# A hand-written instruction planner counts longer instruction fetches and a shorter run of warm-up products, and lays the order of an attention and MoE kernel anew

## The chip, the cores and the metric

The kernel runs on one core of a Trainium2 chip. The metric is the device time of one execution in microseconds (us). Three runs of the kernel before gave 327.25, 327.46 and 327.77 us; the median is 327.46 us. One further execution was profiled; durations in this document come from such profiled executions.

## What is computed

Two layers follow each other. The first is attention with 8 batches, 8 heads and head size 64. Each batch has 32 global tokens and 512 local ones. A global token attends to all 544 tokens; a local token attends to the 32 global tokens and to the local ones at a distance of at most 32.

```python
s_g = scale * np.matmul(q_g, k_all.transpose(0, 1, 3, 2))
out_g = np.matmul(sm(s_g), v_all)
mask = np.abs(pos[:, None] - pos[None, :]) <= window          # window = 32
s_ll = np.where(mask, scale * np.matmul(q_l, k_l.transpose(0, 1, 3, 2)), -1000000000.0)
s_lg = scale * np.matmul(q_l, k_g.transpose(0, 1, 3, 2))
a_l = sm(np.concatenate([s_lg, s_ll], axis=-1))
out_l = np.matmul(a_l, np.concatenate([v_g, v_l], axis=2))
```

The second is a two-layer network over the 4352 token rows of width 512 that come out of the first:

```python
h = x @ w_in                                   # 512 -> 2048
g = h * np.clip(h + 3.0, 0.0, 6.0) / 6.0
return (g @ w_out).astype(np.float32)          # 2048 -> 512
```

## The kernel before, in words

**Work of a batch.** Attention of a batch comes as four pairs of 32-query strips and two global units. A pair takes scores on TensorE (L712 for batches 0 and 1, in 32x32 tiles; L699 later, in tiles of another shape), eight masked maxima on VectorE (L743), eight exponentials on ScalarE (L749), eight 128x128 transposes on TensorE (L758), one copy out of PSUM (L318), the product with the values (L776, 32-column weights) and on VectorE the normalization (L785, L786) and the transpose to the layout of the network (L799, into the tile xt). A global unit takes scores (L824, later L816), a maximum (L831, L832), two exponentials (L836, L837), five transposes (L847) and a copy; both units together take one product with the values (L857). Scores, of pairs and of global units alike, go through one PSUM tile s: the next scores wait until all readers of the last ones are done.

**Network of a batch.** Sixteen column tiles of the first matrix (L907, four matmuls of 128x512 each; in batch 0 in three parts of fewer tokens) go into one of three PSUM buffers m0 to m2; ScalarE takes relu (L918), VectorE the product with it (L914, into gts), which frees the buffer. For each of the four groups of 128 tokens the second matrix takes 16 matmuls of 128x512 in four groups of four (L934), into the same three buffers, copied out by ScalarE or VectorE (L942, L944) and stored by SP. The first L907 of batches 1 to 7 needs all of the batch's xt, so it waits for the batch's last L776 and the L785, L786 and L799 after it. L934 of the batch before can be laid between.

**Loads.** For batches from 2 on, q and k are loaded by DMAs that POOL issues into 32 partitions of rawq and rawk, and SP then issues DMAs inside the memory that copy them to 32 further partitions (a pair for rawq, a pair for rawk; three of the same kind for the global rows, gn). VectorE transposes them from there (L646 for q, L650 for k, four instructions each). POOL also loads v and copies it into vs (L542; ScalarE has some of these copies of batch 0 at L540). SP issues its DMAs in order: a store that waits for its copy holds back what is queued behind it.

**The order.** No order is written out. The kernel adds every step to one of some 50 streams of a planner (class Plan, L34 to L196) with a cost on each engine that may take it, and `lay` (L124) puts steps one after the other on a model of the engines' clocks: at each turn the engine that can start first takes, among the steps that are ready there, the one of lowest rank (the number beside the stream's name, L296 to L299). A step that ScalarE or VectorE may take goes to the one with the smaller end, where VectorE's end counts SPARE later. The order that results is emitted once and is fixed from then on; at run time an engine goes through its own list and waits where a semaphore makes it.

The planner also has an instruction fetch in its model. It counts TensorE's instructions, weight loads and matmuls alike, in blocks of 256 (BLOCK). When the count passes into a new block at a time `when`, the block after it is taken to be there some microseconds later (`self.fetched`, L179); a step that would pass the next border before that time has its rank raised by 20, so that others go first. The 100 products of zeros at the start (stream "pad", L996) have a cost of their own, which the model multiplies by SLOW before COLD (30 us).

Where this document speaks of a place in TensorE's list, it numbers weight loads and matmuls in order; the kernel has 8968 of them, in both versions.

Of the kernel before, what the change touches and what calls it, by code (L numbers as in the profile page):

```python
# [37 lines left out]
class Plan:  # L38
# [4 lines left out]
    BLOCK = 256  # L43
    COLD, SLOW = 30.0, 1.9
    SWITCH, ALONE = 0.097, 0.5
    SPARE, PHASES = 0.5, 9

    def __init__(self, pools, claims):
        self.count, self.fetched, self.mode = 60, 0.0, "full"
# [72 lines left out]
    def lay(self):  # L122
        at = self.at = {n: 0 for n in self.streams}
        clock = {}  # L124
        order = []
        total = sum(len(s) for s in self.streams.values())
        while len(order) < total:
            found, lone = [], []
            for n, ops in self.streams.items():
                if at[n] == len(ops):  # L130
                    continue
                op = ops[at[n]]
                t = self.ready(op, n)
                if t is None:
                    continue
                for e in op.on:
                    if e in op.holds and op.holds[e].end is None:
                        continue
                    start = max(t, clock.get(e, 0.0))
                    cost = self.cost(op, e, start)  # L140
                    rank = self.rank[n](at[n]) if callable(self.rank[n]) else self.rank[n]
                    rank += self.tune.get((n, at[n] * self.PHASES // len(ops)), 0.0)
                    if e == "PE":
                        cost += self.switch(op)
                        if self.stalls(op, start, cost - self.switch(op))[0] > 0.2:
                            rank += 20
                        if op.mode[0] != "full" and self.mode != "full":
                            rank -= 15
                        elif op.mode[0] != "full" and start - t < self.ALONE:
                            lone.append(len(found))  # L150
                    found.append((start, rank, start + cost, n, e))
            if not found:
                raise RuntimeError("no operation can be laid: " + ", ".join(f"{n} {at[n]}" for n in at if at[n] < len(self.streams[n])))
            if len(lone) == 1:
                start, rank, end, n, e = found[lone[0]]
                found[lone[0]] = (start, rank + 12, end, n, e)
            first = min(found)
            e = first[4]
            here = [f for f in found if f[4] == e and f[0] <= first[0] + 0.03]
            start, _, end, n, e = min(here, key=lambda f: (f[1], f[0]))  # L160
            op = self.streams[n][at[n]]
            if len(op.on) > 1:
                own = min(f[1] for f in found if f[3] == n)
                wanted = lambda f: f[4] != e and any(g[4] == f[4] and g[3] != n and g[1] < own and g[0] <= f[0] + 0.05 for g in found)
                start, end, e = min(((f[0], f[2], f[4]) for f in found if f[3] == n and not wanted(f)),
                                    key=lambda f: f[1] + (self.SPARE + self.tune.get(("spare " + n, at[n] * self.PHASES // len(self.streams[n])), 0.0)
                                                          if f[2] == "DVE" else 0.0))
            for b, p, i in self.choose(op, n)[1]:
                b.at, b.slot = p, i
                self.free[p][i] = None  # L170
            at[n] += 1
            if op.landing is not None:
                self.issued.setdefault(e, []).append(op.landing)
            if e == "PE":
                wait, when = self.stalls(op, start, self.cost(op, e, start))
                end += wait
                self.mode = op.mode[1]
                if self.count % self.BLOCK + op.n >= self.BLOCK:
                    self.fetched = when + wait + (7.0 if when < 40.0 else 5.2)  # L179
                self.count += op.n  # L180
            clock[e] = end
            op.end, op.engine = end + op.lat, e
            for b in op.reads:
                b.left -= 1
                b.free_at = max(b.free_at, op.end)
                if b.left == 0:
                    self.free[b.at][b.slot] = b.free_at
            order.append((start, n, op))
        return order
# [3 lines left out]
def kernel(  # L193
# [12 lines left out]
    nc = tc.nc  # L206
# [6 lines left out]
    NDFF = dff // P  # L213
    W = 32
# [12 lines left out]
    PARTS, CG = ((1,), (0,), (2, 3)), 4  # L227
# [38 lines left out]
    vs = tiles("vs", 2, [P, NU, NJ, H, D1], FP16)  # L266
# [16 lines left out]
    zero = tiles("zero", 1, [W, W], FP16)[0]  # L283
# [9 lines left out]
    aps = tiles("a", 1, [P, 2, 512], FP32, pp)  # L293

    plan = Plan(sizes, {})
    for name, rank in (("l0", 0), ("ld", 5), ("lq", -2), ("sh", 0), ("sq", 0), ("st", 3.5), ("g0", 0), ("ga", -9), ("first", -9), ("pad", -30), ("gc", -6), ("gd", 3), ("gp", 3.9), ("cast", -5), ("msk", lambda n: 1 if n < 9 else 1.25), ("tq", lambda n: 0 if n < 8 else 3), ("kg", 0.5), ("vs", 1.5), ("clr", 1),  # L296
                       ("s", 0.5), ("mx", lambda n: 1.2 if n < 33 else 2.7), ("ex", 1.9), ("t", -0.5), ("etc", 0), ("av", -0.7), ("nm", 0.7),
                       ("xp", -0.5), ("gx", 1),
                       ("mf", lambda n: 9 + n * 1e-3), ("ms", lambda n: 9 + (n + len(PARTS) * NDFF + 2) * 1e-3), ("t1", 0), ("gate", -0.7), ("ot", 3)):  # L299
        plan.stream(name, rank)  # L300
    for name in ("l0", "ld", "lq", "sh", "st", "g0", "ga", "sq"):
        plan.stream("dq" + name, 0 if name in ("l0", "ld", "lq") else -1)
# [690 lines left out]

    with tc.manual_schedule():
        clean = plan.add("first", Op(("DVE", 0.1), lambda: nc.vector.memset(zero, 0.0)))
        plan.add("pad", Op(("PE", 4.0), lambda: [nc.tensor.matmul(out=aps[0][0:W, 0, 0:2], lhsT=zero, rhs=zero[:, 0:2], start=True, stop=True) for _ in range(100)], [clean],  # L996
                           n=200, mode=("small", "small")))
        plan.add("first", Op(("DVE", 3.4), setup))
        plan.add("first", Op(("ACT", 2.2), lambda: nc.scalar.activation(out=mxs[1], in_=mxs[0], func=EXP)))
        loads(0, "l0")  # L1000
        v_loads(0, "l0")
        w_in_l = load_w_in()
        made["clear"] = plan.add("clr", Op(("POOL", 2.4), lambda: clear(nc.gpsimd, 1), [made["ident"]]))
        turn_qk(0)
        loads(1, "l0")
        if WORDS > 1:
            g_first(1)
        v_loads(1, "l0")
        w_out_l = load_w_out()
        for u in range(NU):  # L1010
            state[1]["vs"][u, 0][0].deps[0].deps.append(w_out_l[NDFF // 2])
        for b in range(2, B):
            loads(b, "l0" if b == WORDS else "lq")
            if b >= WORDS and (b - WORDS) % NG == 0:
                g_rest(b, "l0" if b == WORDS else "ld")
            v_loads(b, "ld")
            if b < WORDS:
                g_first(b)
        for b in range(B):
            if b:  # L1020
                turn_qk(b)
            pairs_of = [local(b, n, b == 0 and at % 2 == 1, b == 0 and at < HALVES)
                        for at, n in enumerate(range(NI // 2) if b else (1, 0, 2, 3))]
            for one in pairs_of[:HALVES]:
                next(one, None)
            for one in pairs_of:
                next(one, None)
            for s in range(2):
                globe(b, s)
            globe_values(b)  # L1030
        for b in range(B):
            moe_first(b)
            for j in ([i for part in PARTS for i in part] if b == 0 else range(NJ - (b == B - 1))):
                moe_second(b, j)
        moe_global()
        moe_second(B - 1, NJ - 1, 2)
        state[1]["g4"].deps[0].holds = {"POOL": made["strips"][-1][1]}
        for need, op in made["strips"]:
            if need:
                op.holds = {e: state[0]["turned"][need - 1][1] for e in ("ACT", "DVE")}  # L1040
        firsts = [op for b, i, op in units if b == 0 and i < NI]
        firsts[2].holds = {"PE": state[0]["turned"][0][0]}
        firsts[3].holds = {"PE": state[0]["summed"][0]}
        for b, i, op in units:
            at = b - 1 + (i - LEAD) / (NI + 2)
            if at > 0:
                op.deps.append(hold(at))
        for _, _, op in plan.lay():
            op.emit()
# [30 lines left out]
```

## Time and profile before

| what | value |
|---|---|
| median of 3 runs | 327.46 us (327.25 to 327.77) |
| the profiled execution, its own time | 328.56 us |
| its span | 326.8 us, so 1.76 us lie around it |
| granted TensorE clock | 1.00 in every 10 to 20 us up to 300 us, 0.98 after |
| busy in the span | TensorE 305.8 us, VectorE 258.4, ScalarE 238.3, POOL 157.7 |
| TensorE busy in 0 to 10, 10 to 20, 20 to 30, 30 to 40 us | 3.43, 6.05, 8.56, 7.67 us |
| TensorE busy in 40 to 50, 50 to 60 us | 10.00, 7.23 us |
| TensorE busy in each stretch from 60 to 300 us | all of it |

A line of a timeline gives the start in us, the time from the start of the first to the end of the last of the merged instructions, the engine, the line of the kernel, the operation, the tiles (written <- read), the shape and how many; in brackets the idle time before it and what ended it. "issue" there means that the engine waited for nothing that the profile shows. Matmuls are pipelined, so the time from one start to the next start is what a group costs; the ends overlap.

### The profile page before, as it was taken

The page shows a single profiled execution, that of the slowest core. Times are in us where ns is not written, and L with a number is a line of the kernel's source. Part 1 is how long each engine was busy: PE and PEld are TensorE (multiplying, and loading weights), DVE is VectorE, ACT ScalarE, POOL GpSimd, SP SyncE. Part 2 cuts the span into 40 slices and gives each one's busy share as a digit, 9 for nine tenths or more (in the row PEclk, how much of TensorE's full clock was granted, in tenths as well). Part 3 has the DMA queues.
Part 4 walks back from the last instruction along what each step waited for, and adds up shares of the span by engine and source line. Part 5 has one row for each costly group of instructions (what it writes and reads, how often), then busy time and mean ns, then how long its engine had stood idle before and what let it go on. Part 6 is the DMA issues. An engine that isn't in the chain of part 4 may idle for free.

```text
span 326.8 us, 11215 instructions
## 1 busy us (share of the span) xinstructions
PE 305.8 (94%) x4484; PEld 172.8 (53%) x4484; DVE 258.4 (79%) x913; ACT 238.3 (73%) x550; POOL 157.7 (48%) x205
## 2 busy tenths in 40 slices
PE   4477898799999999999999999999999999999995
PEld 4356784454555545555555555555455545556654
DVE  7788996789989897989998999889989985742210
ACT  7999678557895788868876997699759965643221
POOL 9999999029955935665009944963900000000000
PEclk9999999999999999999999999999999999999999
DMA  8999999959952995199949993999111012011223
GB/s 201 180 215 190 188 212 170 230 152 178 200 85 66 140 184 138 46 111 160 217 118 99 226 138 48 148 157 174 33 35 34 2 34 67 0 34 32 65 53 79
DMA packets 104821, 39.54 MB, mean 121 GB/s; under 512 B 91648, under 2 KB 97536, under 8 KB 104768
## 3 DMA queue, kind: packets, MB, share of 16 engines
q0 software_dynamic: 91392, 16.91, 63.9%
q1 hardware_dynamic: 12832, 21.78, 26.8%
q8 instruction: 35, 0.57, 0.7%
q10 hardware_dynamic: 544, 0.13, 0.2%
q14 instruction: 18, 0.15, 0.2%
HBM read 35.13 MB, written 8.91 MB: 135 GB/s over the span
## 4 chain that ended last, share of the span: by engine, by line
PE 86%; POOL 5%; DMA 3%; DVE 2%; issue 2%; ACT 0%; POOLq 0%
PE m L934 37%; PE m L907 35%; PE t L758 4%; DMA xt<-in_q_l_dram 3%; PE a L776 3%; PE s L699 3%; PE t L847 1%; POOL vs L542 1%; PE s L816 1%; POOL v L308 1%; PE a L857 1%; PE s L712 1%; POOL win L308 1%; DVE qt L590 1%; DVE kt L595 1%
## 5 line engine op out<-in xcount | busy, mean ns | idle before, releaser
L934 PE MATMUL m<-wout,gts 128*128 128x512 f16 (+1 forms) x560 | 130.8, 373 | 1.8 <-issue 1.8
L907 PE MATMUL m<-xt,win 128*128 128x512 f16 (+2 forms) x640 | 121.0, 338 | 2.2 <-DVE gts L914 1.2
L914 DVE SCALAR_TENSOR_TENSOR gts<-t,m 128x512 f16<-128x512 f32 x136 | 92.1, 682 | 34.4 <-ACT t L918 33.1
L918 ACT ACTIVATE t<-m 128x512 f32<-128x512 f32 x136 | 81.2, 597 | 34.5 <-PE m L907 31.4
L907 PEld LDWEIGHTS <-win 128*128 128x128 f16 x704 | 70.4, 114 | 48.0 <-issue 3.8
L542 POOL COPY vs<-v 32x1056 f32<-32x1056 f32 (+4 forms) x91 | 81.7, 898 | 29.1 <-DMA v<-in_v_l_dram 24.8
L749 ACT ACTIVATE ex<-sm,mx 128x128 f16<-128x128 f32 x256 | 84.9, 394 | 7.2 <-DVE mx L743 6.5
L934 PEld LDWEIGHTS <-gts 128*128 128x128 f16 x560 | 51.6, 98 | 52.1 <-issue 3.5
L743 DVE CUSTOM_DVE_ANT_0 sm<-s,mask 128x128 f32<-128x128 f32 x240 | 56.2, 285 | 7.2 <-PE s L712 4.1
L308 POOL DMA_DIRECT2D rawq<-in_q_l_dram x12 | 12.6, 1059 | 46.3 <-DVE rec L785 24.3
L318 ACT COPY et<-t 128x1024 f16<-128x1024 f16 x28 | 28.1, 1005 | 8.1 <-PE t L758 8.0
L308 POOL DMA_DIRECT2D v<-in_v_l_dram x32 | 28.2, 896 | 0.0
L942 ACT COPY ot<-m 128x512 f32<-128x512 f32 (+1 forms) x29 | 16.5, 570 | 15.3 <-PE m L934 15.2
L786 DVE TENSOR_TENSOR x<-a,rec 128x512 f16<-128x512 f32 x32 | 22.1, 692 | 1.1
L799 DVE STREAM_TRANSPOSE xt<-x 128x512 f16<-128x512 f16 x32 | 22.5, 704 | 0.1
L758 PEld LDWEIGHTS <-ex 128*128 128x128 f16 x256 | 17.3, 101 | 9.0 <-ACT ex L749 2.7
L743 DVE DVE_READ_ACCUMULATOR2_ANT mx<- 128x1 f32 x256 | 21.3, 83 | 0.0
L758 PE MATMUL t<-ident,ex 128*128 128x128 f16 x240 | 19.9, 225 | 1.5 <-ACT ex L749 1.5
L318 ACT COPY etg<-t 128x640 f16<-128x640 f16 x16 | 11.1, 692 | 10.5 <-PE t L847 10.5
L776 PEld LDWEIGHTS <-et 128*32 128x32 f16 x1024 | 10.0, 98 | 13.1 <-ACT ex L749 4.7
L646 DVE STREAM_TRANSPOSE qt<-rawq 128x512 f16<-128x512 f16 x24 | 15.5, 680 | 0.0
L650 DVE STREAM_TRANSPOSE kt<-rawk 128x512 f16<-128x512 f16 x24 | 15.5, 679 | 0.0
(92 smaller groups left out, 221.5 us busy)
## 6 DMA issues: line engine op xcount, KB each, us to landing
out_dram<-ot SPq DMA_DIRECT2D x62, 128.0 KB, 2.9
vs<-vg SPq DMA_DIRECT2D x32, 132.0 KB, 5.4
v<-in_v_l_dram POOLq DMA_DIRECT2D x32, 128.0 KB, 6.4
rawq<-in_q_l_dram POOLq DMA_DIRECT2D x12, 256.0 KB, 5.8
rawk<-in_k_l_dram POOLq DMA_DIRECT2D x12, 256.0 KB, 6.8
rawq<-rawq SPq DMA_DIRECT2D x12, 254.0 KB, 5.3
rawk<-rawk SPq DMA_DIRECT2D x12, 254.0 KB, 4.9
win<-in_moe_w_in_dram POOLq DMA_DIRECT2D x4, 512.0 KB, 11.3
```

Source lines behind the costliest of these rows:

```text
L308: eng.dma_start(out=o() if callable(o) else o, in_=i() if callable(i) else i)
L318: nc.scalar.copy(out=o(), in_=i())
L542: (nc.gpsimd if op.engine == "POOL" else nc.vector).tensor_copy(out=o(), in_=i())
L743: nc.vector.tensor_tensor_reduce(out=sms[sm.slot], in0=scored(c // 2)[:, z:z + P], in1=mask(m), scale=-scale, scalar=3.0e38, op0=ALU.add, ...
L749: nc.scalar.activation(out=exs[ex.slot][:, un, c, :], in_=sms[sm.slot], func=EXP, scale=-1.0, bias=mxs[mx.slot])
L758: nc.tensor.matmul(out=turned(tp)[:, z:z + P], lhsT=exs[ex.slot][:, un, c, :], rhs=ident, is_transpose=True)
L786: nc.vector.tensor_tensor(out=xs[x.slot].rearrange("p g (a d) -> p g a d", a=2), in0=o[:, :, 0:D].rearrange("p g (d a) -> p g a d", a=2), ...
L799: nc.vector.transpose(out=xts[xt.slot][:, :, n * P:(n + 1) * P].rearrange("p k (t q) -> p t k q", q=W), in_=xs[x.slot].rearrange("p (t k) ...
L907: nc.tensor.matmul(out=mps[ps.slot][:, k * n:(k + 1) * n], lhsT=column_tile(c)[:, m], rhs=x, start=(m == 0), stop=(m == KC - 1))
L914: nc.vector.scalar_tensor_tensor(out=g, in0=shape(t1s[t1.slot][:, 0:all_]), scalar=1.0, in1=shape(mps[ps.slot][:, 0:all_]), op0=ALU.min, o ...
L918: r = plan.add("t1", Op(("ACT", 0.09 + all_ * 0.00083), lambda: nc.scalar.activation(out=t1s[t1.slot][:, 0:all_], in_=mps[ps.slot][:, 0:al ...
L934: nc.tensor.matmul(out=mps[ps.slot][:, 0:n], lhsT=gfn(c), rhs=w_out_t[c // 4][:, c % 4, cols], start=(c == 0), stop=(c == NDFF - 1))
```

## The change

Three numbers of the planner's model change, and nine ranks. No instruction is added or removed apart from who takes a copy; the list of each engine comes out in another order. In the order laid anew ScalarE takes one of the single vs copies of batch 0 instead of five, VectorE eight instead of three, POOL as many as before ahead of its load of batch 1's q; one of the four casts of batch 0's q and k goes from ScalarE to VectorE.

```diff
-    SPARE, PHASES = 0.5, 9
+    SPARE, PHASES = 0.8, 9
...
                 if self.count % self.BLOCK + op.n >= self.BLOCK:
-                    self.fetched = when + wait + (7.0 if when < 40.0 else 5.2)
+                    self.fetched = when + wait + (7.0 if when < 40.0 else 6.2 if when < 62.0 else 5.2)
                 self.count += op.n
...
# ranks, old -> new (all others stay)
-    ("st", 3.5), ("kg", 0.5), ("vs", 1.5), ("ex", 1.9), ("t", -0.5), ("nm", 0.7), ("xp", -0.5), ("t1", 0), ("gate", -0.7)
+    ("st", 2), ("kg", 1.2), ("vs", 3.7), ("ex", 2.7), ("t", 0.2), ("nm", 0), ("xp", -1.2), ("t1", -1.5), ("gate", -1.4)
...
-        plan.add("pad", Op(("PE", 4.0), lambda: [nc.tensor.matmul(out=aps[0][0:W, 0, 0:2], lhsT=zero, rhs=zero[:, 0:2], start=True, stop=True) for _ in range(100)], [clean],
+        plan.add("pad", Op(("PE", 1.45), lambda: [nc.tensor.matmul(out=aps[0][0:W, 0, 0:2], lhsT=zero, rhs=zero[:, 0:2], start=True, stop=True) for _ in range(100)], [clean],
                            n=200, mode=("small", "small")))
```

The streams of these ranks are the stores (st), the copies that complete k (kg), the vs copies (vs), the exponentials (ex), the transposes of a pair (t), the normalization (nm) and the transpose to xt (xp) on VectorE, and relu and gate of the network (t1, gate).

## The prediction

> **What bounds the kernel now.** I read the page first: busy time, then the slices.
>
> ```profile
> PE 305.8 (94%) x4484; PEld 172.8 (53%) x4484; DVE 258.4 (79%) x913; ACT 238.3 (73%) x550; POOL 157.7 (48%) x205
> ```
>
> TensorE is the bound, and busy in the whole of each stretch from 60 to 300 us. No matmul is added or removed, so only holes can move the time. Of those after 37.75 us the timeline of TensorE shows two long ones:
>
> ```profile
> 51.34 0.63 PE L712 MATMUL s<-kt,qt 32*32 32x128 f16 x51
> 52.89 0.30 PE L712 MATMUL s<-kt,qt 32*32 32x128 f16 x13 [0.92 <-issue]
> 53.12 1.04 PE L934 MATMUL m<-wout,gts 128*128 128x512 f16 x4
> ...
> 56.42 0.82 PE L934 MATMUL m<-wout,gts 128*128 128x512 f16 x3
> 59.09 1.25 PE L934 MATMUL m<-wout,gts 128*128 128x512 f16 x5 [1.85 <-issue]
> 60.27 0.43 PE L776 MATMUL a<-vs,et 128*32 128x65 f16 x32
> ```
>
> Both have nothing before them but "issue". Counting weight loads and matmuls in the list, these holes stand at places 1980 and 2236: 256 apart. Smaller ones stand at the same spacing earlier: 20.51, 26.69 and 32.67 us; place 1724 is passed at 46.74 us. From border to border it takes 6.18 and 5.98 us, and (46.74 to 52.89 to 59.09) 6.15 and 6.20 us. So a block of 256 instructions arrives no sooner than about 6.2 us after the border before it, and 64 scores of L712 (128 places in 0.67 us) use up a block quickly. The queue table has 35 packets of that kind, as 8968 instructions in blocks of 256 would need (35.03):
>
> ```profile
> q8 instruction: 35, 0.57, 0.7%
> ```
>
> From start to start the first hole costs 1.78 us for 64 scores that take 0.67 elsewhere (1.11), the second 3.85 us for eight L934 that take 1.83, a change of tile shape included (2.02): **3.13 us**.
>
> The third place that matters is the first L907 of batch 1, which needs the last transpose to xt:
>
> ```profile
> 65.92 0.43 PE L776 MATMUL a<-vs,et 128*32 128x65 f16 x32
> 66.28 0.45 PE L824 MATMUL s<-kt,qg 32*32 32x288 f16 x16
> 66.66 0.45 PE L847 MATMUL t<-ident,eg 128*128 128x128 f16 x5
> 66.95 2.75 PE L934 MATMUL m<-wout,gts 128*128 128x512 f16 x12
> 69.54 0.44 PE L847 MATMUL t<-ident,eg 128*128 128x128 f16 x5
> 69.82 1.89 PE L907 MATMUL m<-xt,win 128*128 128x512 f16 x8
> ```
>
> and VectorE beside it:
>
> ```profile
> 66.45 0.21 DVE L785 RECIPROCAL rec<-a 128x8 f32<-128x8 f32 x1 [0.48 <-PE a L776]
> 66.69 0.69 DVE L786 TENSOR_TENSOR x<-a,rec 128x512 f16<-128x512 f32 x1
> 67.30 0.75 DVE L831 TENSOR_REDUCE top<-s 128x1 f32<-128x576 f32 x1
> 68.08 0.15 DVE L832 TENSOR_SCALAR mx<-top 128x1 f32<-128x1 f32 x1
> 68.15 0.70 DVE L799 STREAM_TRANSPOSE xt<-x 128x512 f16<-128x512 f16 x1
> ```
>
> From the start of the last L776 to the end of L799 at 68.85 are 2.9 us, and TensorE doesn't notice: twelve L934 of batch 0 lie over it.
>
> **The start stays.** The chain of waits fixes it:
>
> ```profile
> 19.71 11.34 DMA xt<-in_q_l_dram
> 31.08 2.08 DVE qt L590
> 35.20 1.98 DVE kt L595 x4
> 37.75 4.69 PE m L907 x56
> ```
>
> POOL issues that load at 19.71 us after 11 vs copies, still 11 in the new list. VectorE gets five more single vs copies and a cast (the single copies took 0.29 to 0.52 us), ScalarE gives up four (0.41); walking both lists with before's durations, VectorE is free at 30.2 us, before the load lands at 31.05. So L907 of place 1390 starts at 37.75 again, which I take as plus or minus 0.4.
>
> **The holes go: -3.13.** I laid the new TensorE list from 37.75 us with before's times from start to start: L934 or L907 of 128x512 0.865 per four (128x256 0.109, 128x128 0.056 each), L712 0.67, L758 0.45, L776 0.36, L847 0.28, L824 0.38, and 0.095 for each entry to a small tile shape. It meets the borders 1724, 1980, 2236 and 2492 at 47.5, 53.85, 60.0 and 66.3 us, 6.2 to 6.35 apart, because the list now puts L934 between the scores. With a block 6.2 us after its border nothing is left but 0 to 0.1.
>
> The Trainium skill ("Runtime: NRT & Kernel Launch", section "Instruction fetch mechanics") says that the fetch comes in 16 KiB blocks of 256 instructions and that crossing a border is mostly hidden. The size agrees with the 256 here; "mostly hidden" doesn't, with 0.92 and 1.85 us idle.
>
> **New starvation before batch 1's first L907: +2.45.** The new list lays all sixteen groups of L934 of batch 0 ahead of batch 1's last L776; before kept two of them and the last of a third back, 12 matmuls. Behind that L776 (place 2510, 67.2 us in my walk with its small delays) come only one L824, one L847 and, at 68.2, the first L907, which is what TensorE would reach without waiting. It waits for VectorE: L785 at 67.2 + 0.53 = 67.75, L786 until 68.6, then in the new list one L650 (k of batch 2, 0.63) and only then L799 (0.63 plus 0.1 to TensorE): 69.95 if L650 can start at once. It waits for the second copy inside rawk. SP issued that copy at
>
> ```profile
> 61.69 0.79 SPq L308 DMA_DIRECT2D rawk<-rawk  x1
> ```
>
> and it landed at 68.7 us. In the new list two stores stand ahead of it, waiting for an L942 at about 57.95; they (1.19), the first copy and three gn copies (2.73) come before it, so it is issued at 62.4 to 62.5. Landing after 7.0 us as before gives 69.4; L650 and L799 then end at 70.6, and L907 starts at **70.65**, 2.45 late. That duration is the nearest row: same copy, same place, the same loads beside it. The other copies of this kind have a median of 4.9 us, which would land at 67.35 and leave 69.95 (1.75 late). The upper end is 71.3, for a copy that lands 0.65 later than reckoned. Behind the late L650 nothing else of TensorE waits so soon.
>
> **Small terms.** L857, two L907 groups on, needs the last etg copy, whose scores come late (L824 of the second unit waits for L836 and L837 of the first): +0.37, between 0 and 0.7. Changes of tile shape: after place 2500 the new list has 121 instead of 115; the whole list from place 1390, laid with the same prices, is +0.45 longer (all its matmuls are the same, so this is switches alone).
>
> **Later batches: 0, between -0.5 and +1.8.** The vs copies of POOL now stand behind the loads of rawq and rawk: by before's durations they are ready 2 us (batch 2) to 8 us ahead of use. At the borders of batches 2 to 7 3.4 to 5 us of L934 lie behind the last L776, more than the 2.9 us chain. In the long L907 stretches a buffer m comes round after three groups (2.6 us), and the product L914 is 0.2 to 0.3 us ahead of that in my walk; VectorE is 88 to 91% busy there. A gain is possible only where a wait stood before, and there is nearly none from 60 us on, hence the small lower end.
>
> **Sum:** -3.13 + 2.45 + 0.37 + 0.45 = +0.14 us. The profiled execution (328.56 us, span 326.8) would become 328.7 (span 326.9); it lies 1.1 above the median of the runs, and I take the difference over: 327.46 + 0.14 = **327.6 us**.
>
> **Rivals.** About 0.2% (0.65 us) is what a measurement of this kernel can tell from no change.
>
> *Faster: the copy lands early.* With 4.9 us, L907 starts at 69.95: -3.13 + 1.75 + 0.37 + 0.45 = -0.56; without the wait of L857 -0.93; if the switches cost half, -1.15: 326.3 to 326.9 us. For it: two stores more ahead leave the queues emptier. Against it: this very copy took 7.0. Chance 0.33.
>
> *Slower: the products come late.* In the L907 stretches of batches 2 to 7 VectorE has the masked maxima of the next batch and one normalization more between the L914s. The point is 0.26 us: if L914 comes later than that, TensorE waits at the third use of each m. At 0.3 us per batch over six batches this is 1.8: 327.6 + 1.8 = 329.4 us, at half the batches 328.5. For it: VectorE's share there. Against it: L914 waited for ScalarE 33.1 us in all before, so it has slack on average. Chance 0.17.
>
> *The change doesn't do what it says: borders elsewhere.* The planner starts its count at 60, and I placed borders by the holes. If blocks come 6.5 us apart when loads are dense, 0.3 to 0.5 us stays at each of three borders: 328.5 to 329.1. Chance 0.10.
>
> *The holes are no block fetch.* Then they are a delay tied to L712 between groups of L934, which all stay: 327.6 + 3.1 = 330.7 us. The equal distances and the 35 packets speak against it. Chance 0.03. (The rule of the Trainium skill weighed above, "Runtime: NRT & Kernel Launch", "Instruction fetch mechanics", would lead here.)
>
> **Chances.** Forecast 0.37: 0.32 of it within 0.65 us of before, 0.05 above. Early copy 0.33, of which 0.03 within. Late products 0.17, borders 0.10, no fetch 0.03: slower. So faster 0.30, same 0.35, slower 0.35. Range 326.2 to 329.3: from the early copy's end to the late products'; left out are 0.03 and the edges of the others.
>
> **What would show it.** Right: no "issue" over 0.2 us on TensorE between 38 and 67 us; L776 of batch 1's last pair at 67.2; an idle time before the first 128x512 L907 of about 2.4 us, released by L799, with an L650 between L786 and L799 whose releaser is a DMA; then TensorE full from 72 us on, its last L934 0.1 to 0.2 us later than before. Wrong: that L907 at 70.0 or before (faster), idle time released by L914 or by relu in the L907 stretches (slower), "issue" at 47, 54, 60 or 66 us (fetch not as reckoned), or L907 of place 1390 not at 37.75 (the start moved).

## The result, and the profile after

The changed kernel takes 329.70 us (median of 20 runs, 328.07 to 333.12); the kernel before, run beside it, 327.75 us (20 runs, 326.58 to 329.59). The ratio is 1.0062, 95% interval 1.0038 to 1.0085: slower by some 2 us, where 327.6 and "no change" were forecast (range 326.2 to 329.3). Its profiled execution took 330.97 us, span 329.2.

The page after, busy time:

```profile
PE 307.8 (94%) x4484; PEld 173.4 (53%) x4484; DVE 257.4 (78%) x914; ACT 238.8 (73%) x549; POOL 157.5 (48%) x205
```

TensorE does the same matmuls and is busy 2 us longer, so part of them ran slower. The timeline of TensorE (start, time, engine, line, tiles, count; idle before in brackets):

```profile
54.02 0.73 PE L712 MATMUL s<-kt,qt 32*32 32x128 f16 x64
...
60.48 0.73 PE L712 MATMUL s<-kt,qt 32*32 32x128 f16 x64
...
67.71 0.42 PE L776 MATMUL a<-vs,et 128*32 128x65 f16 x32
69.23 0.45 PE L824 MATMUL s<-kt,qg 32*32 32x288 f16 x16 [1.09 <-ACT eg L837]
69.61 0.45 PE L847 MATMUL t<-ident,eg 128*128 128x128 f16 x5
71.75 3.29 PE L907 MATMUL m<-xt,win 128*128 128x512 f16 x8 [1.69 <-DVE xt L799]
74.88 0.44 PE L847 MATMUL t<-ident,eg 128*128 128x128 f16 x5
```

The two holes are gone: L712 of the borders (places 1980 and 2236, at 54.32 and 60.55 us, 6.2 apart) have no bracket. In their place TensorE idles 2.8 us between batch 1's last L776 and its first L907, and the first eight L907 then take 3.13 us from start to start where eight take 1.73 in the kernel before. VectorE shows why L907 starts late:

```profile
68.24 0.21 DVE L785 RECIPROCAL rec<-a 128x8 f32<-128x8 f32 x1 [0.41 <-PE a L776]
68.48 0.69 DVE L786 TENSOR_TENSOR x<-a,rec 128x512 f16<-128x512 f32 x1
70.39 0.71 DVE L650 STREAM_TRANSPOSE kt<-rawk 128x512 f16<-128x512 f16 x1 [1.22 <-DMA vs<-vg]
71.03 0.67 DVE L799 STREAM_TRANSPOSE xt<-x 128x512 f16<-128x512 f16 x1
```

L650 stands between L786 and L799 and waits for a DMA, as forecast. The bracket names a copy of vs; what L650 needs is the second copy inside rawk, issued at 63.25 us and landed 7.0 us later, at 70.20. L650 starts 0.19 us after that landing, and 0.19 us after it in e2, e3, e6 and e13 too, so it is this copy that ends the wait. And the table by stretches (busy time of each engine, then granted clock, DMA share, GB/s) shows the slow matmuls:

```profile
70.00:71.00 1.00, 0.06 (x2) 0.00 (x0) 0.61 (x1) 0.69 (x1) 0.00 (x0) 1.00 1.63 197
71.00:72.00 1.00, 0.25 (x1) 0.11 (x1) 1.00 (x3) 0.00 (x0) 0.00 (x0) 0.61 1.74 191
72.00:73.00 1.00, 1.00 (x4) 0.31 (x3) 0.97 (x3) 0.44 (x2) 0.00 (x0) 0.50 2.19 178
73.00:74.00 1.00, 1.00 (x4) 0.42 (x3) 1.00 (x3) 0.78 (x3) 0.00 (x0) 0.50 2.26 172
```

The granted clock fell to 0.50 after the idle stretch, for about 3 us: 1.40 us lost. Nothing of this was in the prediction.

The table below cuts every profiled execution at two places: the first L907 of place 1390 (end of the start) and batch 1's first L907 of 128x512. It holds all 20 profiles. "Holes" are the longest start-to-start steps at places 1980 and 2236, where 0.01 to 0.05 is a plain step after a score and 0.22 one after a 128x512 matmul.

| execution | place 1390 | first L907 of batch 1 | between | from there to the end | steps at 1980, 2236 |
|---|---|---|---|---|---|
| before, first profile | 37.75 | 69.82 | 32.07 | 256.98 | 1.14, 2.23 |
| before (e5) | 38.30 | 68.37 | 30.06 | 256.93 | 1.06, 0.31 |
| before (e11) | 40.44 | 70.27 | 29.84 | 256.93 | 0.94, 0.22 |
| after, first profile | 38.28 | 71.75 | 33.48 | 257.45 (1.40 by the clock) | none |
| after (e6) | 40.59 | 73.46 | 32.86 | 256.04 | none |
| after (e13) | 37.86 | 71.01 | 33.15 | 256.09 | none |
| e1, e14: L799 first | 37.82, 38.75 | 69.52, 70.45 | 31.70, 31.70 | 256.68, 257.25 | none |
| e2: bridge | 39.40 | 73.33 | 33.93 | 256.07 | none |
| e3: turn first | 37.10 | 70.11 | 33.01 | 257.59 (slow clock) | none |
| e4: fetch term undone | 38.99 | 70.04 | 31.06 | 257.06 | 0.16, 0.56 |
| e12: the same, turn first | 38.20 | 68.45 | 30.25 | 257.85 | 0.25, 0.23 |
| e7: three moves | 37.38 | 69.08 | 31.70 | 257.22 | none |
| e8: fetch term alone | 38.01 | 70.38 | 32.37 | 256.82 | none |
| e9: half scores | 37.77 | 65.77 | 28.00 | 256.93 | none |
| e10: one group | 37.78 | 68.19 | 30.41 | 257.81 | 0.15, 1.41 |
| e16: small value | 37.95 | 69.04 | 31.09 | 256.66 | 0.95, 0.85 |
| e17: two values | 39.41 | 70.26 | 30.85 | 255.74 | none |
| e15, e18: two values, turn first | 37.02, 39.14 | 67.87, 69.98 | 30.85, 30.85 | 256.23, 255.62 | none |

### The profile page after: what moved, and what is told of

Its sections match the earlier page's. It is cut to its first block, busy times and chain, and to the rows that moved or that the text cites. A ratio compares the mean times of both kernels' runs of the same rounds, so it can differ in the third digit from the quotient of the medians.

```text
span 329.2 us, 11212 instructions
## 1 busy us (share of the span) xinstructions
PE 307.8 (94%) x4484; PEld 173.4 (53%) x4484; DVE 257.4 (78%) x914; ACT 238.8 (73%) x549; POOL 157.5 (48%) x205
## 4 chain that ended last, share of the span: by engine, by line
PE 84%; DVE 8%; DMA 4%; ACT 2%; issue 1%; SPq 0%; DVEq 0%
PE m L907 36%; PE m L934 33%; PE t L758 4%; PE a L776 3%; PE s L699 3%; DMA rawk<-rawk 2%; DVE sm L743 2%; PE s L816 1%; PE t L847 1%; DMA win<-in_k_l_dram 1%; DVE kt L595 1%; DVE x L786 1%; DMA vs<-vg 1%; PE s L712 1%; PE a L857 1%; DVE qt L590 1%
## 5 line engine op out<-in xcount | busy, mean ns | idle before, releaser
L934 PE MATMUL m<-wout,gts 128*128 128x512 f16 (+1 forms) x560 | 131.2, 373 | 0.0
L907 PE MATMUL m<-xt,win 128*128 128x512 f16 (+2 forms) x640 | 125.7, 342 | 2.7 <-DVE xt L799 1.7
L914 DVE SCALAR_TENSOR_TENSOR gts<-t,m 128x512 f16<-128x512 f32 x136 | 92.0, 681 | 40.7 <-ACT t L918 39.5
L907 PEld LDWEIGHTS <-win 128*128 128x128 f16 x704 | 70.1, 115 | 47.5 <-issue 5.2
L934 PEld LDWEIGHTS <-gts 128*128 128x128 f16 x560 | 52.0, 98 | 51.8 <-issue 1.7
L318 ACT COPY et<-t 128x1024 f16<-128x1024 f16 x30 | 30.2, 1006 | 8.2 <-PE t L758 8.1
L942 ACT COPY ot<-m 128x512 f32<-128x512 f32 (+1 forms) x31 | 17.7, 570 | 14.7 <-PE m L934 14.4
L786 DVE TENSOR_TENSOR x<-a,rec 128x512 f16<-128x512 f32 x32 | 22.1, 691 | 1.1
L799 DVE STREAM_TRANSPOSE xt<-x 128x512 f16<-128x512 f16 x32 | 22.4, 701 | 0.1
L758 PEld LDWEIGHTS <-ex 128*128 128x128 f16 x256 | 17.5, 101 | 8.2 <-ACT ex L749 1.4
L758 PE MATMUL t<-ident,ex 128*128 128x128 f16 x240 | 19.7, 225 | 0.6 <-ACT ex L749 0.6
L776 PEld LDWEIGHTS <-et 128*32 128x32 f16 x1024 | 10.0, 98 | 13.5 <-ACT t L918 4.6
L650 DVE STREAM_TRANSPOSE kt<-rawk 128x512 f16<-128x512 f16 x24 | 15.3, 674 | 1.2 <-DMA vs<-vg 1.2
```

The lines of the kernel that those rows point to most:

```text
L318: nc.scalar.copy(out=o(), in_=i())
L758: nc.tensor.matmul(out=turned(tp)[:, z:z + P], lhsT=exs[ex.slot][:, un, c, :], rhs=ident, is_transpose=True)
L786: nc.vector.tensor_tensor(out=xs[x.slot].rearrange("p g (a d) -> p g a d", a=2), in0=o[:, :, 0:D].rearrange("p g (d a) -> p g a d", a=2), ...
L799: nc.vector.transpose(out=xts[xt.slot][:, :, n * P:(n + 1) * P].rearrange("p k (t q) -> p t k q", q=W), in_=xs[x.slot].rearrange("p (t k) ...
L907: nc.tensor.matmul(out=mps[ps.slot][:, k * n:(k + 1) * n], lhsT=column_tile(c)[:, m], rhs=x, start=(m == 0), stop=(m == KC - 1))
L914: nc.vector.scalar_tensor_tensor(out=g, in0=shape(t1s[t1.slot][:, 0:all_]), scalar=1.0, in1=shape(mps[ps.slot][:, 0:all_]), op0=ALU.min, o ...
```

## The experiments

Theory after the result: the change trades holes that cost little in most runs against a bare border before batch 1's L907, with the slow clock on top in some runs. Rivals: the start, L650 alone, the ranks in later batches. Kernels that were measured together shared a chip and the runs of the kernel before; its median is given each time. Most edits move steps in the list that the planner returns, ahead of its emission:

```python
laid = [op for _, _, op in plan.lay()]
of = plan.streams
def move(moved, what):          # put steps right behind another step
    for o in moved:
        laid.remove(o)
    at = laid.index(what) + 1
    laid[at:at] = moved
```

**e1 and e14, L799 first** (on the changed kernel): `move([of["xp"][7]], of["nm"][8])`.

> The changed kernel with one step moved: batch 1's last L799 stands ahead of the first L650 in VectorE's list. Theory A (L650's wait for the copy inside rawk holds L799, and so the first L907 of batch 1; the long idle then halves the granted clock): L907 starts at 69.9 to 70.1 us instead of 71.75, the idle of 1.69 us before it goes, the granted clock stays 1.00 from 70 to 80 us; median 1.7 us less plus the clock's share in some runs, 327.3 to 327.8 with the kernel before at 327.7 (ratio 0.999 to 1.000). Rival B (another wait ends just as late: L857 for etg, or a product for kt of batch 2): L907 early, but TensorE idle as long elsewhere; ratio 1.004 or more.

Measured 328.76 us (before 328.11; ratio 1.0013, 0.9978 to 1.0048). L907 started at 69.52 us, earlier than A's 69.9 to 70.1, and the clock stayed at 1.00. The profile bears A out, the median does not: it lies about 1 us above A's. On that chip the kernel before spread from 326.60 to 332.63 us, so the pair was run again beside the changed kernel (e13, e14):

> The changed kernel, unchanged, beside the variant with L799 first on one chip: ratio 1.005 to 1.008, idle of 1.0 to 1.8 us before batch 1's first L907, released by L799, with L650 between L786 and L799.

> The changed kernel with L799 ahead of the first L650, beside the changed kernel on one chip. Theory A (L650's wait and the slow clock behind it are the larger part of the loss): 1.2 to 2.2 us under the changed kernel's median, ratio to the kernel before 1.000 to 1.003, no run with a mean clock under 0.996. Rival B (the start and the missing worth of the holes are the larger part): under 1 us below the changed kernel.

Changed kernel 328.95 (ratio 1.0043, 1.0017 to 1.0069), with L799 first 328.35 (1.0012, 0.9990 to 1.0033), before 327.69: only 0.6 us, as rival B said. The changed kernel's ratio is a little under the 1.005 to 1.008 expected. The timeline of TensorE in e14 shows what became late next:

```profile
70.45 1.89 PE L907 MATMUL m<-xt,win 128*128 128x512 f16 x8
72.99 0.70 PE L847 MATMUL t<-ident,eg 128*128 128x128 f16 x5 [0.66 <-ACT eg L836]
```

L907 came 1.4 us earlier counted from place 1390 (31.70 against 33.15), but the second unit's L831 still stood behind L650, its L847 came late, and the rest grew by 0.6 to 1.2 us. So on this chip L650's wait is not the larger part of the loss.

**e2, bridge** (on the changed kernel):

```diff
+ bridge = Op(("PE", 1.5), lambda: [nc.tensor.matmul(out=mps[of["mf"][48].takes[0].slot],
+     lhsT=w_out_t[0][:, 0, 0:P], rhs=w_out_t[1][:, 0, :], start=True, stop=True) for _ in range(8)])
+ laid.insert(laid.index(of["t"][10]) + 1, bridge)
```

> The changed kernel with eight more products of 128x512 ahead of batch 1's first L907, into the PSUM buffer that this L907 overwrites; their results are not used. The wait for L799 stays. Theory A (the idle stretch halves the clock): L907 still starts at about 71.7 us, but the first eight L907 take 1.73 us instead of 3.13, granted clock 1.00; no run above 330, median 0.5 to 1.0 below the changed kernel's 329.7: 328.6 to 329.1 (ratio 1.003 to 1.004). Rival B (the slow clock is not due to the idle, but falls at a time): granted clock 0.5 for 3 us again, ratio 1.006. Rival C (the products delay L907): slower than the changed kernel by up to 1.7.

Measured 329.13 us (328.87 to 329.52 apart from the profiled run, which took 331.14 with a start 1.1 us later than after's), before 328.11; the ratio is 1.0000 (0.9967 to 1.0033), under A's 1.003 to 1.004. Two views of e2, the timeline of TensorE (L1056 is the bridge) and the stretches:

```profile
71.03 1.89 PE L1056 MATMUL m<-wout,wout 128*128 128x512 f16 x8
73.33 1.89 PE L907 MATMUL m<-xt,win 128*128 128x512 f16 x8 [0.41 <-DVE xt L799]
```

```profile
72.00:73.00 1.00, 0.92 (x5) 0.31 (x3) 1.00 (x2) 0.00 (x0) 0.00 (x0) 1.00 1.71 184
73.00:74.00 1.00, 0.67 (x4) 0.36 (x4) 0.97 (x3) 0.00 (x0) 0.00 (x0) 1.00 2.13 147
```

L907 waits for L799 as before, yet runs at full clock, and L907 to the end is 256.07: A in the profile. Of the changed kernel's 41 runs 16 have a mean granted clock of 0.995 or less, of the bridge's 13 none, of the 24 with L799 first none. The idle stretch is the cause in the changed kernel. The kernel before has such runs too, 22 of its 139 beside the experiments; none of these was profiled, so what idles there is not known.

The stretch from batch 1's last L776 to L907 doesn't end in the slow clock each time: 3.68 us with 0.8 us of products in it (first profile of the changed kernel) and 3.21 us (e3) did, 3.34 us (e13) did not. The clock records in the traces show a reason. The 0.50 at L907 lasts 3.41 us in both executions, and the full clock, from its first record on, lasts 13 times 3.41 us in these two and 86 to 88 times in the other 18: the clock changes only at the borders of stretches of 3.41 us. In the 20 traces TensorE was busy for 1.39 us or less in 22 such stretches, and each was followed by 0.50 (20 of them at the end of the execution); in the other 1725 it was busy for 1.46 us or more, and none was. The idle time of that first profile lay for the most part in one stretch with 1.17 us of work, that of e3 in one with 1.10; in e13 a border fell into it, and the emptier stretch had 2.07.

The Trainium skill ("TensorE: Matmul & The Clock Gate", "Part 1: The HAM clock gate") states a free-running window of about 3.4 us, after which an idle TensorE falls to half clock. The 3.41 us and the 0.50 agree with it; but the stretches before a fall were not empty here, with 1.10 and 1.17 us of work.

**e3, turn first** (on the changed kernel): `move([of["s"][6]], of["t"][1])`.

> The changed kernel with one step moved: the second turn of batch 0 (eight L758 into an m buffer) stands ahead of the first L824 in TensorE's list, as in the kernel before, so that it lies in L824's wait. Theory A (the start is late because this turn, its copy on ScalarE and L776 were put behind L824's wait): the next L776 at about 25 us instead of 26.40, VectorE free before the load of xt lands (31.05), the L907 of place 1390 at 37.75 instead of 38.28; 0.5 us less, ratio 1.004 to 1.005. Rival B (VectorE's five further vs copies and the cast make the start late): place 1390 stays at 38.2 to 38.3, ratio 1.006.

Measured 328.51 (before 328.11; ratio 1.0013, 0.9980 to 1.0047, under what A and B said). Place 1390 came at 37.10 us, the L776 at 25.24: A by its profile. But the start turned out to move from execution to execution in every kernel: 37.75 to 40.44 in the kernel before, 37.82 to 40.59 in lists with the changed kernel's start, 37.02 to 39.14 with the turn first. In the two latest, e11 of the kernel before and e6 of the changed one, half of an early L776 waits 1.52 us for a copy of vs. One profile can't price the start.

**e4, fetch term undone** (on the changed kernel), **and e8, fetch term alone** (on the kernel before):

```diff
- (7.0 if when < 40.0 else 6.2 if when < 62.0 else 5.2)     # e4
+ (7.0 if when < 40.0 else 5.2)
- (7.0 if when < 40.0 else 5.2)                             # e8
+ (7.0 if when < 40.0 else 6.2 if when < 62.0 else 5.2)
```

> The changed kernel without the longer fetch term (5.2 us again for all borders after 40 us), laid anew. Its TensorE list passes the borders 1724, 1980 and 2236 faster and keeps three groups of L934 between batch 1's last L776 and its first L907. Theory A (holes are the fetch of blocks, 6.2 us apart; the fetch term used up the L934 that covered the border of the batch): two holes marked issue come back, about 1.1 us at place 1980 and 2.7 at 2236, no idle before batch 1's first L907 and no slow clock; span 1.2 us over the kernel before with the late start in it, 328.7 to 329.2 (ratio 1.003 to 1.005). Rival B (the ranks, not the fetch term, removed the holes): no hole over 0.2 us, ratio 0.993 to 0.997. Rival C (the ranks, not the fetch term, caused the starvation): idle before that L907 again.

> The kernel before with the longer fetch term alone (6.2 us for borders from 40 to 62 us), laid anew. Its start is that of the kernel before to place 1400; its L799 stands ahead of the L650; no L934 is left between batch 1's last L776 and its first L907. Theory A (the term trades holes for a bare border): no hole at 1980 and 2236, one of about 1.7 us at place 2492 (its walk reaches it 4.5 us after the border before), idle of 1.0 to 1.5 us before the first L907 of batch 1 at 70.6 to 71.2; ratio 0.998 to 1.002. Rival B (the fetch term alone is a gain, the ranks spoilt it): ratio 0.993 to 0.996. Rival C (the term alone makes the whole loss): ratio 1.005 to 1.008.

e4: 329.07 against 328.11, ratio 1.0016 (0.9982 to 1.0049), under the expected 1.003 to 1.005. e8: 329.24 against 327.53, ratio 1.0056 (1.0034 to 1.0078). So the fetch term alone makes most of the loss (rival C of e8). The ranks without it cost little, between -0.6 and +1.6 us by e4's interval, and the two together are near the changed kernel's 1.0043 to 1.0073. In e8 no L650 is in the way, and L907 is late all the same:

```profile
67.40 0.43 PE L776 MATMUL a<-vs,et 128*32 128x65 f16 x32
67.75 0.45 PE L824 MATMUL s<-kt,qg 32*32 32x288 f16 x16
68.13 0.45 PE L847 MATMUL t<-ident,eg 128*128 128x128 f16 x5
70.38 1.02 PE L907 MATMUL m<-xt,win 128*128 128x512 f16 x4 [1.79 <-DVE xt L799]
```

The bare border costs 1.79 us without any DMA: L785, L786, L831 and L799 are a chain of 2.9 us, and no L934 covers it. A's hole at place 2492 did not come (that block took 4.78 us or less after its border), and in e4 the holes were 0.1 and 0.5 us instead of 1.1 and 2.7: the two blocks took 5.1 and 4.0 us there instead of 6.2. The next one took 8.2 us and left a hole of 0.2 us at 66.19.

**e5 and e11, the kernel before again.**

> The kernel before, unchanged, for a second profile. Theory A (the two holes are as long as the fetch of a block takes in that execution): holes marked issue at places 1980 and 2236 again, but of other lengths, 1.0 to 4.5 us together; place 1390 within 0.4 us of 37.75, since the load of xt, not VectorE, sets it. Rival B: the holes are the same 3.1 us to 0.2.

> The kernel before for a third profile. Theory A: hole at place 1980 of 0.8 to 1.2 us, and at place 2236 0 to 0.5 us (a block 4 to 4.7 us after its border). Theory P: 1.9 us at place 2236 as in the first profile.

The timeline of TensorE in e5:

```profile
53.36 0.29 PE L712 MATMUL s<-kt,qt 32*32 32x128 f16 x13 [0.84 <-issue]
...
56.89 2.00 PE L934 MATMUL m<-wout,gts 128*128 128x512 f16 x8
58.82 0.36 PE L776 MATMUL a<-vs,et 128*32 128x65 f16 x24
```

The first hole is there (0.84 us), the second has shrunk to 0.1 us inside the eight L934, which take 1.93 us from start to start where the first profile has 3.85. The block of place 2236 came 4.28 us after that of 1980; in e11, where no hole shows, 4.19 us after it or sooner; in the first profile 6.20. Theory A for the holes. Its start was wrong: place 1390 lay at 38.30 (e5) and 40.44 (e11), and in neither does the chain of waits before it lead through the load of xt.

The trace also has the packets of the instruction queue (q8), 16 KB each, and they show what these holes are. In the 20 profiles TensorE has 37 idle times of over 0.05 us marked issue. Every one stands 180 to 190 places behind a multiple of 256 and ends 1.2 to 1.7 us after the end of such a packet. So they are block fetches, and what differs is when the packet starts: for the block of place 2236 it starts 3.72 us after place 1980 in the first profile, and 1.1 to 2.0 us after it in each of the 19 others. The first profile's second hole was the exception.

**e9, half scores** (on the kernel before): in `scores`, for batch 1 from its second pair on,

```diff
- for bb in range(2):
+ for bb in range(1 if b == 1 and n else 2):
...
-     start=(bb == 0), stop=(bb == 1))
+     start=(bb == 0), stop=(bb == 1 or (b == 1 and n > 0)))
```

> The kernel before with half of the products of L712 left out in the last three pairs of batch 1 (the second half of the sum over the head), so those scores are not the reference's; 96 matmuls and as many weight loads fewer, 1.0 us of TensorE. The order stays, the blocks of 256 are passed 7.2 and 5.4 us apart instead of 5.1 and 4.1, so no hole is left by a fetch of 4 to 6.2 us. It measures what the holes cost in the median run. Theory A (the first hole about 1.1 us, the second near nothing in most runs): 1.0 plus 1.2 us faster than the kernel before, ratio 0.992 to 0.994. Theory P (3.1 us in most runs, as predicted): ratio 0.986 to 0.989.

The timeline of TensorE in e9 at places 1980 and 2236, with no idle time before them:

```profile
54.04 0.42 PE L712 MATMUL s<-kt,qt 32*32 32x128 f16 x32
...
59.24 0.42 PE L776 MATMUL a<-vs,et 128*32 128x65 f16 x32
```

Measured 325.44 against 327.63, ratio 0.9926 (0.9898 to 0.9955): 2.2 us less, 1.0 of it the scores themselves, so the holes cost 1.2 us in the median (0.5 to 2.3 by the interval), not 3.1.

**e6 and e7, changed kernel and three moves.** e7 adds to the two moves `move([of["ot"][3]], of["ex"][66])`.

> The changed kernel, unchanged, beside its variants on one chip. Ratio 1.003 to 1.008; about 4 runs in 10 with a mean granted clock of 0.995 or less and 1.4 us longer than the others. In its profile place 1390 lies between 37.8 and 39.4 us, as it follows the first loads of k, and an L650 stands between L786 and L799 and waits for the copy inside rawk.

> The changed kernel with three steps moved: L799 ahead of L650 (as in the first experiment), the second turn of batch 0 ahead of the first L824 (as in the third), and batch 0's last L942 on ScalarE behind the first unit's L836 and L837. Theory A (start, wait for L650 and slow clock are the loss): place 1390 at 37.1 to 37.9, first L907 of batch 1 at 69.0 to 69.8, no slow clock; median 1.2 to 2 us under the changed kernel's on the same chip, ratio to the kernel before 0.996 to 1.000. Rival B (the loss lies in later batches): within 0.5 us of the changed kernel.

Changed kernel 330.55 (ratio 1.0073, 1.0047 to 1.0100), three moves 328.12 (1.0010, 0.9986 to 1.0034), before 327.53. The 2.4 us between the two are more than A's 1.2 to 2, because four of e6's nine runs have the slow clock; the median of its other five is 328.79, and 0.7 us are left. Theory A in outline: with the slow clock, all of the loss but 0.6 us is in these places. The ratio ended just above the expected interval's upper end, and place 1390 of e6 lay at 40.59, later than expected.

**e12, fetch term undone and turn first:** e4 with e3's move.

> The changed kernel without the longer fetch term, as in the fourth experiment, and with the second turn of batch 0 ahead of the first L824, as in the third: what is left of the change are the other ranks. Theory A (the two moves of the fetch term and of the turn are the loss): place 1390 at 37.0 to 37.8, ratio 0.999 to 1.001, 0.5 to 1 us under the fourth experiment. Rival B (the ranks cost elsewhere too): ratio 1.002 or more.

328.62 against 327.63, ratio 1.0020 (0.9992 to 1.0048): inconclusive, at the lower edge of rival B. Place 1390 lay at 38.20, later than A said.

**e10, one group** (on the kernel before): each of batch 0's L934 groups from the fourth to the fourteenth takes the place of the one ahead of it, and the fourth goes ahead of the third L712 of batch 1; then

```diff
+ move([of["t"][11]], of["mf"][49])
+ move([of["etc"][11]], of["t1"][17])
+ move([of["av"][9]], of["ms"][14])
```

> The kernel before with one more group of L934 ahead of batch 1's third L712 and one group less behind its last L776, and the second unit's L847 with its copy and both units' L857 moved behind two L907. Theory A: the hole at place 1980 falls from 1.1 to 0.2 us, a part of it (0.5 to 0.9) comes back at place 2236, the first L907 of batch 1 starts 0.3 to 0.9 us earlier than in the kernel before from the same start, with less than 0.3 us idle before it: ratio 0.997 to 0.9995. Rival B (the fetch of the second block takes 6.2 us in most runs): no gain, ratio 1.000 to 1.002. Rival C (L799 now late): idle of over 0.5 us before that L907, ratio 1.000 to 1.003.

328.31 against 327.63, ratio 1.0025 (0.9999 to 1.0052), a miss. The hole left place 1980 and came back whole at place 2236, since place 2236 was now reached earlier; and from batch 1's first L907 to the end it took 257.81 us where the kernel before takes 256.93, which stays unexplained:

```profile
57.57 0.23 PE L712 MATMUL s<-kt,qt 32*32 32x128 f16 x1 [1.19 <-issue]
```

**e16, small value, and e15, e17, e18, two values.** e16 has, on the kernel before, `6.2 if when < 46.0 else 4.6` in place of 5.2, which touches only the borders after 46 us. e17 has, on the changed kernel,

```diff
- (7.0 if when < 40.0 else 6.2 if when < 62.0 else 5.2)
+ (7.0 if when < 40.0 else 6.2 if when < 52.0 else 4.6)
```

and e15 and e18 have e3's move with it.

> The kernel before with 4.6 us instead of 5.2 for borders after 46 us, laid anew; its start is unchanged. Places 1980 and 2236 are passed as in the kernel before, so the holes stay (1.1 us and up to 0.5), three groups of L934 stay behind batch 1's last L776, and the list has 0.43 us less by its own prices (fewer changes of tile shape). Theory A (these sums hold): ratio 0.998 to 1.000. Rival B (a new wait behind place 2600): ratio over 1.002.

> The changed kernel with two values for the fetch instead of one (6.2 us for borders from 40 to 52 us, 4.6 us later), laid anew, and the second turn of batch 0 ahead of the first L824. Two groups of L934 stay behind batch 1's last L776, and L799 stands ahead of the L650. Theory A (a block takes 6 us first, then 4 to 4.8): no hole over 0.3 us at places 1980 and 2236, idle of 0.3 to 0.8 us before the first L907 of batch 1, 31 us or less from place 1390 to it; 0.5 to 1.0 us faster than the kernel before, ratio 0.997 to 0.9985. Rival B (a block takes 6 us at 2236 too): a hole of 1.5 us there, ratio 1.001 to 1.003.

> The changed kernel with two values for the fetch (6.2 us for borders from 40 to 52 us, 4.6 us later), laid anew; the second turn of batch 0 stays behind the first L824. Theory A (start and fetch add up): place 1390 at 37.8 us or later, from there to batch 1's first L907 31 us as with both; ratio 0.997 to 1.000, 0.4 to 1.0 us above the kernel with both. Rival B (the turn gives nothing in the median): within 0.3 us of it.

> The changed kernel with two values for the fetch and the second turn of batch 0 ahead of the first L824, a second time: ratio 0.993 to 0.998, place 1390 at 37.0 to 38.2 us.

e16: 327.65 against 327.69 (0.9996, 0.9970 to 1.0022), as A said, with a second hole of 0.6 us, a little over its 0.5. e15: **326.63 against 327.69, ratio 0.9954 (0.9927 to 0.9981)**. On another chip, beside a median of 328.51 of the kernel before, e17: 327.06 (0.9958, 0.9928 to 0.9988), e18: 326.56 (0.9938, 0.9907 to 0.9969). So two values beat the kernel before, and on e15's chip the changed kernel (328.95) too; the turn adds about 0.5 us (327.06 to 326.56), inside both intervals. In e18 place 1390 lay at 39.14, later than expected. On that other chip 12 of the 23 runs of the kernel before took 328.5 us or more, and the other 11 have a median of 327.07, while none of the 24 runs of e17 and e18 took over 328.03: there most of the gain is that the long runs are missing. The timeline of e15:

```profile
52.77 0.74 PE L712 MATMUL s<-kt,qt 32*32 32x128 f16 x64
...
57.50 0.74 PE L712 MATMUL s<-kt,qt 32*32 32x128 f16 x64
...
64.84 0.42 PE L776 MATMUL a<-vs,et 128*32 128x65 f16 x32
...
65.87 1.89 PE L934 MATMUL m<-wout,gts 128*128 128x512 f16 x8
```

Place 2236 comes 4.57 us after 1980 without a hole, and the two L934 groups saved by that lie over the border. It gained more than A expected, and the profiles don't account for it in full: from place 1390 to the end they take 286.5 to 287.1 us, the kernel before 286.8 to 287.0 in two profiles and 289.05 in the first. What is left must lie in the start and in runs unlike these profiles, such as runs with a long second hole; how often those come is not known.

## Why the prediction was wrong

- **"The holes go: -3.13"** is the step that failed. They went, but were worth 1.2 us in the median (e9). The mechanism held; the size came from one execution in which the second block took 6.20 us, against 4.28 and at most 4.19 in two others. The warning was in the numbers: the profiled execution lay 1.1 us above the median of the runs, and "I take the difference over" carried those 1.1 us into both kernels, though much of them was the very hole that was to be removed.
- **"New starvation: +2.45", L907 at 70.65.** Right. From place 1390 it was to be 32.90 us; measured 32.86, 33.15 and 33.48. The cause, L650 behind the copy inside rawk (6.5 to 7.0 us), was seen in the profile; taken away, the bare chain and L847 keep most of the loss (e8, e14). One count is short: behind batch 1's last L776 the kernel before has not 12 L934 but 20, 8 of them after the first L907. They now lie ahead of that L776, which moves 1.73 us of work from the rest to the way there; the walk had them there, so the sum is untouched.
- **The small terms and the later batches.** A sum of +0.14 with L907 0.83 later (70.65 for 69.82) leaves a rest 0.69 us shorter; it is 0.84 to 0.94 shorter, the clock's 1.40 taken off, so these terms fit. Of the rivals, the early copy did not come; from 60 us on no L914 released a wait of TensorE, against the late products; and no hole stood at any border after 38 us, against the other two.
- **"The start stays", 37.75 plus or minus 0.4.** 38.28, 40.59 and 37.86, so outside in one of three by 0.1 and in one by 2.4; but the kernel before also varies from 37.75 to 40.44. So the place is undecided from profiles. The reason given, the load of xt, did not hold: in all three profiles of the changed kernel, and in e5 and e11, the chain of waits does not go through that load. VectorE, walked to be free at 30.2 us, was free at 31.74, since L776 came 1.7 us late behind L824's wait.
- **Missing: the slow clock**, 1.4 us in the profile, and a lower mean clock in 16 of 41 runs against 22 of 139 of the kernel before. The idle stretch was priced at its length alone.

With the holes at 1.2 instead of 3.13 the same sum gives -1.2 + 2.45 + 0.37 + 0.45 = +2.1 us, or 329.6. That this is next to the measured 329.70 is in part luck, since the slow clock isn't in the sum: without its runs the median of the 20 is 329.01, and the medians show about +1.3 (chip of e13: 328.86 against 327.6; chip of e6: 328.79 against 327.5). The 0.8 us between +2.1 and +1.3 stay open.

## What to carry to other kernels

Before a stall's price goes into a sum, see whether it is as long in other executions; a profiled time far above the median is a sign that it isn't, and the excess must not be carried over to both kernels. Work that can fill a wait is spent only once: a longer modelled latency pulls it ahead, so ask which later wait it was covering. And an idle stretch of TensorE of some 3 us can cost more than its length, if the clock drops behind it (1.4 us here).

## What the runs showed of the hardware

The fetch of a TensorE block has no fixed time. Where a hole shows it, it took 5.1 and 5.2 us (e4, e12) and 5.9 to 6.1 (three profiles of the kernel before) from place 1724 to 1980; 4.0 (e4), 4.28 (e5), 4.8 (e10, e16) and 6.20 us from 1980 to 2236; and 8.2 us (e4) from there to the next border. In e12 the second one took 3.45 us or less. In five executions the time from 1980 to 2236 went with the packets of the software queue in that stretch (6.20 us with about 5500, 4.8 with 4070 and 3980, 4.28 with 3050, 4.0 with 1190). But a longer stretch holds more packets anyway, and elsewhere the load does not order the times: a DMA share of 1.15 near 20 us went with 6.18 us, and from 1724 to 1980 shares of 2.35 and 2.37 went with 5.13 and 6.12. Why a packet of the instruction queue starts late was not tested.

The granted clock changed in steps of 3.41 us, and fell to 0.50 behind every step with TensorE busy for 1.39 us or less and behind none with 1.46 or more (20 traces). Its records begin at 25.67 us in the first profile of the kernel before, so the 1.00 that the table of the kernel before has ahead of that is an absence of records: eight L758 took 0.82 us from start to start at 23.29 us and 0.45 at 53.99.

The start of one and the same kernel varied by up to 2.7 us.
